# Real parts of eight squarings and two coefficient sums moved from VectorE to float32 identity matmuls on TensorE, with every written-out instruction order replaced

## The chip, the cores and the metric

The kernel runs on one NeuronCore of a Trainium2 chip. The metric is the device time of one execution in microseconds (us). Three executions of the kernel before took 405.08, 403.68 and 402.94 us; the median is 403.68 us. The engines are called by the profile's names: PE (TensorE matmuls, with PEld for weight loads), DVE (VectorE), ACT (ScalarE), POOL (GpSimd) and SP (the queue that issues nearly all DMAs; SPq in the trace).

## The reference

The input x has 2048 rows of 512 values. Four layers follow one another, each added to x after a layer norm: A, B, A, B.

```
x = x + A(layernorm(x));  x = x + B(layernorm(x));  x = x + A(layernorm(x));  x = x + B(layernorm(x))

A: q, k, v = x @ wqkv, 32 heads of 16; each position looks at W = 8 positions, 0, 2, ..., 14 rows back
   softmax over the 8 logits, weighted sum of v, then @ wo
B: dt = exp(log_dt);  A = A_re + i A_im;  Bc, Cc likewise          (512 channels x 128 states)
   P[d,n,l] = exp(dt A[d,n] l),  l = 0..2047
   K[d,l]   = Re sum_n Cc[d,n] P[d,n,l] dt Bc[d,n]
   y = causal convolution of x with K along l (by FFT of length 4096), plus Dskip * x
```

K does not depend on x and is the same in both B layers, so it is made once.

## The kernel before

The work is staged as: generation of K together with the front of the first A layer (function `k_gen`, 0 to about 110 us), the core of the first A layer (`LayerA.core` with l = 0, about 110 to 190 us), the first B layer (`FftB.run` with ORDER0), the front of the second A layer (ORDERF), the core of the second A layer (CORE1) and the second B layer (ORDER1). In each stage a string of letters gives the order in which pieces of work are recorded; a letter calls the next piece of its kind. Each engine executes its own instructions strictly in the recorded order, and waits at the first one whose operands are not ready. SP likewise issues its DMAs one after another in recorded order, so a DMA that is recorded earlier holds up those behind it.

**Generation.** K is formed from powers of z = exp(dt A). The squarings z -> z^2 run for k = 0 to 10: `square(k)` (token s, ACT) squares the real and the imaginary plane into the buffer `ws`; `double(k)` (token i, DVE) makes the new imaginary part 2 re im; `differ(k)` (the next token i, DVE) makes the new real part re^2 - im^2. Planes are 128 x 512 in float32; a z of two planes is the tile `sq_z`, with two buffers. `power(k)` (token b, ACT) copies z to bf16, for k = 3 to 7 into `pow_t` and otherwise into `B_t`; `power_neg` makes the negated imaginary plane. `c_part` (token C) forms the complex product C B in six DVE instructions: for each of the two parts two products into t1 and t2, and one sum into `c_t`. `b_part` (token M) multiplies powers into the table `B_t`, and `levels` (tokens T and U) builds four tables `A_t` from `pow_t`, all on DVE. The products of the tables (token p, PE, line 1268) are copied out by ACT into `kgs` (token x, line 1276). Interleaved with it are the layer norm of x (statistics a, inverse deviation W, applications y and z on ACT and DVE), the transposes of x (token t, PE, line 1196) and the K and Q projections (tokens k and q, PE, line 1206, copied out by ACT under K and Q). When the last `kgs` copy is done, `k_store` sends K to `kd_dram` in 24 DMAs on SP (line 1290).

**Core of an A layer.** m multiplies q with k shifted by the 8 distances (`mult`, DVE, line 342, four per block of rows q = 0 to 3; the first three of layer 0 are done at the end of generation as tokens X); l sums them over a head on PE; x, e, r, n, T are the softmax; v projects V (`v_proj`, PE, line 398, evicted by ACT in line 400) in the order even rows, then odd rows. After the eighth and the sixteenth v, two DMAs (lines 403 and 404) write the shifted rows that later products read:

```
if a >= 14:
    b = a - 14
    nc.sync.dma_start(v[1:113, b:14:2, :], v[0:112, 16 + b:30:2, :])
    nc.sync.dma_start(v[113:128, b:14:2, :], v[112:127, 16 + b:30:2, :])
```

P multiplies the softmax with v (`pv_mult`, DVE, line 467, tile `pav`, one per row in the order 0, 2, 1, 3, 4, ...): row 0 and row 2 read even rows of `v_ext`, row 1 reads odd rows. S and V sum on PE, O is the output projection. Digits and capital letters are events. In layer 0, event 1 is `k_half_load(0)` and event 6 is `k_half_load(1)`: each loads one half of the channels of K back from `kd_dram` into a tile `k_rl` with 18 DMAs on SP (lines 1357 and 1373). In layer 0 the eighth v also starts the four loads of `wo` (line 308) and of the first block of x (line 1455), the sixteenth v those of the other three blocks. The order string of layer 0 before is

```
CORE0 = vmvvvlmqlxmvvvemlvqrlmqvnTmlvxqqlmevlrvmmvvvvnPllPqxmSqTeO0mPlVrP15SOS2PnOPVPOSml4qOOlb3mV78lPPC...
```

so that both events 1 and 6 stand behind the sixteenth v.

Of the kernel before, what the change touches and what calls it, by code (L numbers as in the profile page):

```python
# [10 lines left out]
ACT = mybir.ActivationFunctionType  # L11
ALU = mybir.AluOpType
# [8 lines left out]
P = 128  # L21
# [25 lines left out]
isCbCiCbsiMaiCCbsiMiGGsbcCbMaTMiiMisMbiMbsGbMiGbiMTbcsibTTaiTcbTsbMTiiGbTGGsTMGciaiMTGMcabMGMaTM  # L47
asaMMGMlalTiWMlaaiyTbayiyTMawaMytatMTelkaeMsqMkdliqMaMKMaMMqMqWMlbQQMMMqMyHykUUakpKkyyttkaxUUpKU
kaUUUUaqUUxeUQppqHkdxxKUqeQTkTaUTklqT3paTqlKWTkQTplqkyqx3Ty3QKxT3TTpqlkTpyyHqWEUxktQlKtkUzkekeTK
zUUUkkzkUztKkKtkkTUpexUUKUEkUkeUkUKpKUokxkpxpKUkUxxkqUKEpxoqkkUpUUxopXXXKQpZxxZZ  # L50
"""
ORDER0 = """
KD KA KA KA KD KA KD KA KD KA KD kA KA kD KA KD UA KD UA UA UD KA kA kD kA UD
UA UD UA kD kA kD u UD u u UA m m m UA u u UD u UA m kD UA kD UA m
m u UA u m kA u kD u m kD u kD kA kA yA m YA m yD u yA u m m m
u u yA m m u YA m yA w000D yD yA YD yA w010D YA yD yA
# [3 lines left out]
yA h00 YA h01 v100A v110D h10 a0 z12A p0 z11A n0D h11 w001A w011A S a1 p1 T0 E01A z13A E00D n1G H2  # L60
P02 a2 P00 Q00 p2 T1 E10D E11D P01 P11 P12 n2D H3 a3 P13 T2 P10 E20D E21D P03 p3 P21 P22 n3D
P23 T3 E30D E31A P20 x1
"""
ORDER1 = """
UA UD UA UD UA UA UD UA UD UD u u m m u u m m UA u UA UD m UA u u
UD UA u m m u u m m u YD m u YA YA m u yD m yA u u m m u w001A
m m yA yA w000D YA yD yA YD w011D yA yD w010D yA yD yA v101A v103D v113A v102D v112D v111D v110A v100A
# [919 lines left out]
NROW = 641  # L987


def k_gen(tc, nc, a_consts, ins, kd, la, x_v, lnst, zero, b_consts):  # L990
# [3 lines left out]
    with ExitStack() as ctx:  # L994
# [55 lines left out]
        a_rest()  # L1050
        ws = sp.tile([P, 3, 4 * P], F32, name="ws")
# [3 lines left out]
        cur = {0: sp.tile([P, 2, 4 * P], F32, name="sq_z", tag="sq_z", bufs=2)}  # L1055
        a_re, turn = cur[0][:, 0], ws[:, 2]
# [17 lines left out]
        nc.vector.tensor_tensor(cur[0][:, 1], a_re, sn, ALU.mult)  # L1074
        nc.vector.tensor_tensor(cur[0][:, 0], a_re, cs, ALU.mult)

        def square(k):
            nc.scalar.activation(ws[:, 0:2], cur[k][:], ACT.Square)

        def double(k):  # L1080
            cur[k + 1] = sp.tile([P, 2, 4 * P], F32, name="sq_z", tag="sq_z", bufs=2)
            nc.vector.scalar_tensor_tensor(cur[k + 1][:, 1], cur[k][:, 0], 2.0, cur[k][:, 1], ALU.mult, ALU.mult)

        def differ(k):
            nc.vector.tensor_tensor(cur[k + 1][:, 0], ws[:, 0], ws[:, 1], ALU.subtract)  # L1085

        def planes(k):
            return cur[k][:].rearrange("p r (c x) -> p r c x", c=NCH)
# [4 lines left out]
        def power(k):  # L1093
            copy = copy_by(ENGK["b"][k + max(0, min(k - 3, 5))])
            if 3 <= k <= 7:
                copy(Pw[:, :, k - 3, 1::2, :].rearrange("p c r x -> p r c x"), planes(k))
            else:
                copy(Bt[:, :, :, B_L.index(1 << k), :], cur[k][:].rearrange("p r (q g) -> p r q g", g=4))
# [481 lines left out]
```

## Time and profile before

| what | value |
|---|---|
| time, three executions | 402.94, 403.68, 405.08 us |
| the profiled execution | span 402.6 us from first to last instruction; its own time is not listed beside it |
| DVE busy | 383.5 us, 95% of the span |
| PE busy | 328.0 us (matmul ends are modelled) |
| ACT busy | 321.8 us |
| POOL busy | 59.1 us |
| DVE busy from 10 to 150 us, summed over the windows | 138.4 us of 140 |
| DVE busy from 350 to 402 us | 45.58 us of 52 |

The page gives busy times per engine, the span in 40 slices, the chain of waits that ended last, and the costliest groups of instructions. The trace behind it can be asked for single engines in order of time: start, duration, engine, line, operation, output and inputs. Starts of neighbouring instructions on DVE and ACT are closer together than the listed durations, since one begins while the last one drains: three float32 DVE instructions in a row begin at 9.81, 10.41 and 11.00 us and are listed with 0.67 to 0.68 us each.

### The profile page before, as it was taken

How to read it: one execution, taken by the hardware profiler on the slowest of the kernel's cores; microseconds unless marked ns; L12 is line 12 of the kernel's file. 1: busy time of each engine (PE TensorE's matmuls, PEld its weight loads, DVE VectorE, ACT ScalarE, POOL GpSimd, SP SyncE). 2: the span in 40 equal slices, each digit the busy share in tenths (PEclk: the TensorE clock that was granted, in tenths of full speed). 3: DMA queues.
4: the chain of work that ended last, by engine and by line, in shares of the span. 5: the costliest groups of instructions: out<-in, count | busy, mean ns of one | idle time of the engine just before them, and what ended most of it. 6: DMA issues, size and time to landing. Idle time of an engine off the chain costs nothing.

```text
span 402.6 us, 14781 instructions
## 1 busy us (share of the span) xinstructions
PE 328.0 (81%) x6527; PEld 230.3 (57%) x6527; DVE 383.5 (95%) x460; ACT 321.8 (80%) x557; POOL 59.1 (15%) x75
## 2 busy tenths in 40 slices
PE   3000059999999989999998889999999998997895
PEld 2000026657735656756987888543456666566885
DVE  6999999999999999999999998979899999989994
ACT  7999888898656578988999987674666677989974
POOL 9402400000199500200600000100000001000000
PEclk9999997999999999999999999999999999999999
DMA  7952711115013875259236685730063019504606
GB/s 219 395 143 37 81 52 50 44 27 117 3 43 76 214 210 160 55 173 384 93 112 232 228 285 166 280 114 2 0 170 94 3 39 383 161 2 134 186 14 202
DMA packets 62323, 54.17 MB, mean 135 GB/s; under 512 B 33869, under 2 KB 50738, under 8 KB 60978
## 3 DMA queue, kind: packets, MB, share of 16 engines
q1 hardware_dynamic: 62250, 53.22, 43.5%
q8 instruction: 51, 0.84, 0.9%
q14 instruction: 14, 0.11, 0.1%
q10 hardware_dynamic: 8, 0.00, 0.0%
HBM read 30.15 MB, written 13.24 MB: 108 GB/s over the span
## 4 chain that ended last, share of the span: by engine, by line
PE 36%; DVE 31%; ACT 17%; issue 8%; DMA 5%; SPq 2%; POOL 1%; DVEq 0%; ACTq 0%; POOLq 0%
DVE pav L467 11%; PE pq L398 6%; PE pk L1268 5%; ACT a1s L791 5%; PE pp L1206 4%; DVE t L847 3%; PE pq L223 3%; DVE prod L342 3%; PE pp L282 3%; PE L L350 2%; ACT ub L860 2%; DVE B_t L1110 2%; DVE sq_z L1085 2%; DMA v_ext<-v_ext 2%; DMA kf_ring<-kf_dram 2%
## 5 line engine op out<-in xcount | busy, mean ns | idle before, releaser
L467 DVE TENSOR_TENSOR pav<-attn,v_ext 128x4096 bf16<-128x4096 bf16 (+1 forms) x34 | 72.4, 2168 | 0.4 <-DMA v_ext<-v_ext 0.3
L342 DVE TENSOR_TENSOR prod<-qT,kT_ext 128x4096 bf16<-128x4096 bf16 x29 | 67.0, 2341 | 1.4 <-PE L L350 0.9
L1196 PE MATMUL pt<-ident,x_blk 128*128 128x128 bf16 x64 | 5.9, 241 | 42.8 <-DVE x_blk L197 38.6
L1110 DVE TENSOR_TENSOR A_t<-A_t,pow_t 128x1024 bf16<-128x1024 bf16 (+4 forms) x46 | 38.3, 870 | 0.3
L492 PEld LDWEIGHTS <-pav 64*128 64x128 bf16 x1664 | 26.2, 95 | 13.5 <-DVE pav L467 8.6
L503 PE MATMUL pq<-wop,oT 128*128 128x512 bf16 x128 | 32.9, 379 | 0.7 <-ACT oT L494 0.7
L860 ACT CAST ub<-pb 128x1024 bf16<-128x1024 f32 x32 | 32.1, 1079 | 1.2 <-PE pb L809 1.2
L492 PE MATMUL po<-ident,pav 64*128 64x64 bf16 x1664 | 29.3, 190 | 4.2 <-DVE pav L467 3.2
L400 ACT CAST v_ext<-pq 128x512 bf16<-128x512 f32 x32 | 18.8, 586 | 16.2 <-PE pq L398 16.2
L809 PE MATMUL pb<-a1s,w_sb 128*128 128x64 bf16 x768 | 27.4, 193 | 5.0 <-ACT a1s L791 1.7
L398 PE MATMUL pq<-wv,xnT 128*128 128x512 bf16 x128 | 30.6, 380 | 0.0
L1206 PE MATMUL pp<-xnT,kT_ext 128*128 128x512 bf16 x96 | 27.1, 411 | 4.3 <-ACT kT_ext L1211 2.3
L1196 PEld LDWEIGHTS <-x_blk 128*128 128x128 bf16 x64 | 4.6, 107 | 44.8 <-DVE x_blk L197 38.8
L809 PEld LDWEIGHTS <-w_sb 128*128 128x128 bf16 x768 | 24.9, 98 | 7.2 <-issue 5.2
L791 ACT CAST a1s<-pb 128x1024 bf16<-128x1024 f32 x29 | 28.2, 1059 | 0.8 <-PE pb L802 0.8
L1268 PEld LDWEIGHTS <-A_t 128*64 128x64 bf16 (+1 forms) x512 | 22.9, 107 | 4.5 <-DVE B_t L1110 0.3
L1268 PE MATMUL pk<-B_t,A_t 128*64 128x84 bf16 (+1 forms) x512 | 24.6, 206 | 0.0
L791 DVE CAST a1s<-pb 128x1024 bf16<-128x1024 f32 x19 | 22.6, 1217 | 1.4 <-PE pb L802 1.3
L223 PE MATMUL pq<-xnT,kT_ext 128*128 128x512 bf16 x96 | 23.9, 380 | 0.0
L225 ACT CAST qT<-pq 128x512 bf16<-128x512 f32 x24 | 14.1, 586 | 9.3 <-PE pq L223 9.2
L509 ACT ACTIVATE x_sb<-pq 128x512 bf16<-128x512 f32 x24 | 14.3, 594 | 8.7 <-PE pq L503 8.7
L398 PEld LDWEIGHTS <-xnT 128*128 128x128 bf16 x128 | 11.6, 98 | 15.3 <-issue 3.0
(259 smaller groups left out, 897.0 us busy)
## 6 DMA issues: line engine op xcount, KB each, us to landing
w_sb<-w_dram SPq DMA_DIRECT2D x8, 1024.0 KB, 7.8
w_dram<-xnT SPq DMA_DIRECT2D x1, 4096.0 KB
kf_ring<-kf_dram SPq DMA_DIRECT2D x13, 256.0 KB, 4.8
kf_ring<-kf_dram SPq DMA_DIRECT2D x26, 128.0 KB, 4.3
v_ext<-v_ext SPq DMA_DIRECT2D x4, 784.0 KB, 6.6
x_blk<-in_A_x_dram SPq DMA_DIRECT2D x4, 512.0 KB, 4.1
kT_ext<-in_A_wqkv_dram SPq DMA_DIRECT2D x4, 512.0 KB, 9.2
x_sb<-in_A_x_dram SPq DMA_DIRECT2D x4, 512.0 KB, 5.3
```

Of the source, the lines that this page charges most:

```text
L223: nc.tensor.matmul(pq[:], lhsT=self.wqk[:, dt, ft * P:(ft + 1) * P], rhs=self.xnT[:, dt, q * 512:(q + 1) * 512], start=(dt == 0), stop=(dt ...
L342: nc.vector.tensor_tensor(pr, self.qT[q][:, ft].unsqueeze(1).to_broadcast([P, W, 4, P]), kap, ALU.mult)
L398: nc.tensor.matmul(pp[:], lhsT=xnT[:, dt, a * P:(a + 1) * P], rhs=wv[:, dt, :], start=(dt == 0), stop=(dt == NDT - 1))
L467: nc.vector.tensor_tensor(pv[:, i], attn[:, n % 4].unsqueeze(2).to_broadcast([P, W, DH // parts, H]), vap, ALU.mult)
L492: nc.tensor.matmul(po[:, h, 0, i * nt + ft, :], lhsT=pvf[rows, i, w, ft * P:(ft + 1) * P], rhs=ident[rows, rows], start=(w == 0 and ft + i ...
L503: nc.tensor.matmul(pw[:], lhsT=oT[:, ftp, :], rhs=self.wo[:, ftp, :], start=False, stop=(ftp == NDT - 1))
L791: (self.nc.scalar.copy if eng == "act" else self.nc.vector.tensor_copy)(dst, src)
L809: nc.tensor.matmul(p2[:, j, :], lhsT=self.w2[:, ec * EC + j, :], rhs=a1s[:, ec * EC + j, :], start=True, stop=True)
L860: nc.scalar.copy(ub[:], p2)
L1110: return lambda: nc.vector.tensor_tensor(*args)
L1206: nc.tensor.matmul(pps[kind, b, ft][:], lhsT=la.wqk[:, dt, c:c + P], rhs=la.xnT[:, dt, b * 512:(b + 1) * 512], start=(dt == 0), stop=(dt = ...
L1268: nc.tensor.matmul(o, lhsT=lhs, rhs=Bt[:, ri, c * CH + ql].rearrange("p b g -> p (b g)"), start=(not half and j % 4 == 0 and ri == 0), sto ...
```

## The change

The real part of the squarings with k = 3 to 10 is formed on PE. `ws` holds the two squares in float32; a float32 identity times the first and a negated float32 identity times the second are accumulated in one PSUM bank, and that bank is the real plane from then on. So `square`, `power` and `double` read the real plane from PSUM and the imaginary one from SBUF, and what was one ACT instruction over both planes becomes two. For the first three squarings nothing changes. The two sums of `c_part` are made in the same way, with an ACT copy to `c_t` behind each; the second pair of products is written to a part of `kT_ext`. The two float32 identities are made by POOL behind its other start-up work. The six raw input tiles now lie in the two q tiles (their DMAs are the same, in the same order), and `sq_z` has separate rings for one and two planes.

All order strings are new. The number of pieces of each kind, and the engine of each, are the same as before in every string. In CORE0, event 6 (the load of one half of K) now stands before the odd v, and in the built program its 18 DMAs stand on SP ahead of the two that shift the odd rows of `v_ext`.

```diff
 ORDERK = """
+siCCbisbiisCCCiibsMGCiiMbMMMMsibbbMTMicMMcsabbiisTTbbTTTTiiccTaiGTTsbGbGTTTibMMMasGiiGGaacGaTGMM
+GGbMMMMasallMMMMaaMTaaiiaaMaWlbsMMMaiyyyyilltWbweMMMMMMMMtdkHeqlyyqUUUkUKpUUyykkpQkkKxtaxkkKtpaK
+UUUdapaaUUqqUUUHxaaTTTqq3TTx33l3TTEppQQalTTeeTqWqqQqqQxxqqqllTTQQTTpkyyyypkkkHKKWUUUtxxtekkUelUU
+kkppKKxxzzzzkkkpEKkUUUttkKkepKekkkkUKUUUExxUUUUUUUkKkpokkKKoqoqQXXkkxpKpxpZZXZxx
 """
...
 CORE0 = """
-vmvvvlmqlxmvvvemlvqrlmqvnTmlvxqqlmevlrvmmvvvvnPllPqxmSqTeO0mPlVrP15SOS2PnOPVPOSml4qOOlb3mV78lPPC
-SOdxS6eOrPSPPOSnwaOPSBPOSaOS9bOfAPdbFPOtVftEGDSaafaOH
+vvvmmlvvmxqqllev0vrmmlvvlnTmvmvvvll6xeqPPvvvqqrmmS3lnVlOOqqmx1TPP4qS2SOOm5P7llPVemmSO8PBrCPllbVx
+nOOeSPPrSOnSP9POOASPSOSPPOdSOaaffVbwbOPttdEaaSfaHOGDF
 """
 CORE1 = """
-0m1l2ml3mvvqlmvlvqmxmqvlqqvemllvmrqvlnmTmqxqlmvvelvvvvmPvPqvrlnlTqSmOSxmPqlPeSPOmSOSlOPrlSOqPSPO
-SnmPOOlbxSOPePVbPrdSnPdfOVfaOPwSfPOSfOSbafOPdfaSttfaOa
+0vml12mqmlq3vlqmmlxvvlemmvvrnlqqqlvmTmlqqlxmmvqvlvvmlmevvrvvvPSPlnqOxqSmTOPPlSPOSlSeqOPOrPSSmmlb
+POOSdnPfflOxSePafbVPPdrOnSOVPPfOSPOSbaOPSfdtOfaSfatOaw
 """
...
+SQ_PE = 3
...
         raw = {}
+        q0, q1 = (la.qT[b][:].rearrange("p t a q -> p (t a q)") for b in range(2))
         for name in ("A_im", "A_re", "B_re", "B_im", "C_re", "C_im"):
-            raw[name] = sp.tile([P, 4, N], BF16, name="raw_" + name)
-            nc.sync.dma_start(raw[name][:], ins[name].rearrange("(t p) n -> p t n", p=P))
+            home = (q0, q1)[len(raw) // 4]
+            raw[name] = home[:, len(raw) % 4 * 512:(len(raw) % 4 + 1) * 512].rearrange("p (t n) -> p t n", n=N)
+            nc.sync.dma_start(raw[name], ins[name].rearrange("(t p) n -> p t n", p=P))
...
         a_rest()
+        ident32 = sp.tile([P, P], F32, name="ident32")
+        nident32 = sp.tile([P, P], F32, name="nident32")
+        nc.gpsimd.tensor_copy(ident32[:], ident[:])
+        nc.gpsimd.tensor_copy(nident32[:], la.c["nident"][:])
...
         def square(k):
-            nc.scalar.activation(ws[:, 0:2], cur[k][:], ACT.Square)
+            if k <= SQ_PE:
+                nc.scalar.activation(ws[:, 0:2], (im[k] or z0)[:], ACT.Square)
+                return
+            for r in range(2):
+                nc.scalar.activation(ws[:, r], cur[k][r], ACT.Square)
 
         def double(k):
-            cur[k + 1] = sp.tile([P, 2, 4 * P], F32, name="sq_z", tag="sq_z", bufs=2)
-            nc.vector.scalar_tensor_tensor(cur[k + 1][:, 1], cur[k][:, 0], 2.0, cur[k][:, 1], ALU.mult, ALU.mult)
+            z = sp.tile([P, 1 if k >= SQ_PE else 2, 4 * P], F32, name="sq_z", tag=f"sq_z{k >= SQ_PE}", bufs=2)
+            nc.vector.scalar_tensor_tensor(z[:, 0 if k >= SQ_PE else 1], cur[k][0], 2.0, cur[k][1], ALU.mult, ALU.mult)
+            im[k + 1] = z
 
         def differ(k):
-            nc.vector.tensor_tensor(cur[k + 1][:, 0], ws[:, 0], ws[:, 1], ALU.subtract)
+            if k < SQ_PE:
+                cur[k + 1] = im[k + 1][:, 0], im[k + 1][:, 1]
+                nc.vector.tensor_tensor(cur[k + 1][0], ws[:, 0], ws[:, 1], ALU.subtract)
+                return
+            re = pst.tile([P, 4 * P], F32, name="pt")
+            nc.tensor.matmul(re[:], lhsT=ident32[:], rhs=ws[:, 0], start=True, stop=False)
+            nc.tensor.matmul(re[:], lhsT=nident32[:], rhs=ws[:, 1], start=False, stop=True)
+            cur[k + 1] = re[:], im[k + 1][:, 0]
 
         def power(k):
...
+            for r, z in enumerate(cur[k]):
+                if 3 <= k <= 7:
+                    copy(Pw[:, :, k - 3, 1 + 2 * r, :], z.rearrange("p (c x) -> p c x", c=NCH))
+                else:
+                    copy(Bt[:, r, :, B_L.index(1 << k), :], z.rearrange("p (q g) -> p q g", g=4))
...
+        def c_sum(q, t):
+            pc = pst.tile([P, 4 * P], F32, name="pt")
+            nc.tensor.matmul(pc[:], lhsT=ident32[:], rhs=t[0], start=True, stop=False)
+            nc.tensor.matmul(pc[:], lhsT=(ident32 if q else nident32)[:], rhs=t[1], start=False, stop=True)
+            nc.scalar.copy(c0[:, q], pc[:])
+
+        prods = [(t1[:], t2[:]), [la.kT[:, 3, a:a + 8, :].rearrange("p a q -> p (a q)").bitcast(F32) for a in (14, 22)]]
+
         def c_part():
-                yield tt(nat(t1[:]), T[x0], T[y0], ALU.mult)
-                yield tt(nat(t2[:]), T[x1], T[y1], ALU.mult)
-                yield tt(c0[:, q], t1[:], t2[:], op)
+                t = prods[q]
+                yield tt(nat(t[0]), T[x0], T[y0], ALU.mult)
+                yield tt(nat(t[1]), T[x1], T[y1], ALU.mult)
+                yield lambda: c_sum(q, t)
```

ORDERK before, and the strings ORDER0, ORDERF and ORDER1, which are new as well, are left out of this cut.

More of the change, by code (lines that the diff above doesn't have):

```diff
@@ L1054, in k_gen @@
         t2 = sp.tile([P, 4 * P], F32, name="t2")
-        cur = {0: sp.tile([P, 2, 4 * P], F32, name="sq_z", tag="sq_z", bufs=2)}
-        a_re, turn = cur[0][:, 0], ws[:, 2]
+        z0 = sp.tile([P, 2, 4 * P], F32, name="sq_z", tag="sq_zFalse", bufs=2)
+        cur = {0: (z0[:, 0], z0[:, 1])}
+        a_re, turn = cur[0][0], ws[:, 2]
         p_im = turned_by("A_im", by_dt)
@@ L1110, in tt @@
             return lambda: nc.vector.tensor_tensor(*args)
-        def c_part():
-            for q, (x0, y0, x1, y1, op) in enumerate((("C_re", "B_re", "C_im", "B_im", ALU.subtract),
-                                                      ("C_re", "B_im", "C_im", "B_re", ALU.add))):
-                yield tt(nat(t1[:]), T[x0], T[y0], ALU.mult)
-                yield tt(nat(t2[:]), T[x1], T[y1], ALU.mult)
-                yield tt(c0[:, q], t1[:], t2[:], op)
+        def c_sum(q, t):
[4 more added lines that the diff above has]
+        prods = [(t1[:], t2[:]), [la.kT[:, 3, a:a + 8, :].rearrange("p a q -> p (a q)").bitcast(F32) for a in (14, 22)]]
+        def c_part():
+            for q, (x0, y0, x1, y1) in enumerate((("C_re", "B_re", "C_im", "B_im"), ("C_re", "B_im", "C_im", "B_re"))):
+                t = prods[q]
+                yield tt(nat(t[0]), T[x0], T[y0], ALU.mult)
+                yield tt(nat(t[1]), T[x1], T[y1], ALU.mult)
+                yield lambda: c_sum(q, t)
         def bmul(src, by, dst):
```

45 lines of the change are left out of this document (21 added, 24 removed).

## The prediction

> **What bounds the kernel now.** I read the page first, then the groups of the first 110 us by shape, then the single engines in order of time: POOL and ACT around 13 us, SP from 100 to 200 us, DVE from 98 to 150 us.
>
> ```profile
> PE 328.0 (81%) x6527; PEld 230.3 (57%) x6527; DVE 383.5 (95%) x460; ACT 321.8 (80%) x557; POOL 59.1 (15%) x75
> DVE  6999999999999999999999998979899999989994
> ACT  7999888898656578988999987674666677989974
> ```
>
> DVE is the bound of nearly the whole span; in generation ACT is almost as full (slices 2 to 5). So work taken off DVE counts only while nothing else makes DVE wait.
>
> ```profile
> L1085 DVE TENSOR_TENSOR sq_z<-ws 128x512 f32<-128x512 f32 x11 | 7.5, 683 | 0.1
> L1110 DVE TENSOR_TENSOR c_t<-t,t 128x512 bf16<-128x512 f32 x2 | 1.5, 728 | 0.0
> L1078 ACT ACTIVATE ws<-sq_z 128x1024 f32<-128x1024 f32 x11 | 11.5, 1048 | 0.0
> L1098 ACT CAST B_t<-sq_z 128x1024 bf16<-128x1024 f32 x7 | 7.3, 1039 | 1.4 <-DVE sq_z L1085 1.2
> ...
> 60.96 2.72 PE pp L1206 x6
> ...
> 69.27 0.97 PE pp L1206 x4
> ```
>
> The first four lines are what the change edits (duration of one in ns before the last bar). The last two, from the chain of waits, are the nearest prices for the new matmuls: a bf16 matmul of 512 columns takes 2.72/6 = 0.45 us where the windows show a granted clock of 0.50 (60 to 66 us) and 0.97/4 = 0.24 us where they show 1.00.
>
> ```profile
> 14.06 0.52 POOL L128 TENSOR_SCALAR slot_mask<-iota_slot_mask 4x16 bf16<-4x16 int32 x1
> ...
> 110.01 16.16 SPq L1290 DMA_DIRECT2D kd_dram<-kgs  x24
> 127.55 0.69 SPq L403 DMA_DIRECT2D v_ext<-v_ext  x1
> 128.29 0.94 SPq L404 DMA_DIRECT2D v_ext<-v_ext  x1
> 129.28 4.08 SPq L308 DMA_DIRECT2D wop<-in_A_wo_dram  x4
> 133.40 0.59 SPq L1455 DMA_DIRECT2D x_sb<-in_A_x_dram  x1
> 137.07 0.64 SPq L403 DMA_DIRECT2D v_ext<-v_ext  x1
> 142.12 0.61 SPq L1357 DMA_DIRECT2D k_rl<-kd_dram  x1
> 142.78 12.49 SPq L1373 DMA_DIRECT2D k_rl<-kd_dram  x17
> ...
> 103.41 6.69 DVE L342 TENSOR_TENSOR A_pr<-qT,kT_ext 128x4096 bf16<-128x4096 bf16 x3
> 135.75 4.89 DVE L467 TENSOR_TENSOR pav<-attn,v_ext 128x4096 bf16<-128x4096 bf16 x2
> 146.10 6.68 DVE L467 TENSOR_TENSOR pav<-attn,v_ext 128x4096 bf16<-128x4096 bf16 x3
> ```
>
> Call E the end of the last kgs copy (110.0) and X the start of the first logit product on DVE (103.4). SP does nothing useful for the attention until its 24 stores of K are out: the even rows of v_ext start at E+17.5 and, with the 6.9 us to landing that the DMA view gives, are there at E+24.9, just before the first pav (135.75 = E+25.7). The odd rows are issued at E+27 and are there before the third pav (146.1).
>
> **The change part by part.** *DVE, generation.* Eight subtractions and two sums go. Their starts lie 0.60 us apart, so 10 x 0.60 = 6.0 us (6.9 by listed durations). Nothing is added; a product read from PSUM already costs the same (0.68).
>
> *ACT, generation.* One 1024-wide instruction takes 0.95 us start to start; two of 512 take 0.49 (from PSUM, lines 1072) and 0.52. That is +0.06 for each of 7 squares and 8 power copies, and two copies to c_t add 0.98: +1.9 us in all.
>
> *PE, generation.* Twenty float32 matmuls of 512 columns, in ten pairs; no row shows one. Lower end: one warm bf16 row each, 0.48 a pair. Upper end: each operand is twice as wide as any that PE is given here, so four part products at the cold row, 8 x 0.45 = 3.6 a pair. I take 2.8, between four warm (1.9) and four cold (3.6), because PE ran cold from 60 to 66 us after pauses of 1 to 2 us and the pairs will have such pauses. The Trainium skill, page "FP8 and Floating Point Precision", TensorE Precision Notes, gives float32 four passes, which no run here shows; by it my upper end is the price of a cold pair.
>
> *What waits for the pairs.* In the built order ACT's first c_t copy stands ahead of the power of z^4 and the fourth square, and needs the identities that POOL makes behind slot_mask, ready by about 15.2 and 15.7 us (two instructions like ident, 0.56). The pair then ends at 15.2+2.8 = 18.0; ACT is free at 14.7: a wait of 3.3. Then each square waits for the pair of the square before. From the start of one first-half square its pair begins 0.6 later, so a step is at least 3.4 us; where ACT has less of its own work between two squares it waits: 0.9 before square 4, 0.4 before 5, 0.8 before 6, none after. DVE's doubling waits for that first-half square too (both read the same bank): 2.9 before doubling 4, 1.6 before doubling 7, and 1.5 in the first steps. So DVE idles about 6.0 there against 1.6 before, and X = 103.4 - 6.0 + 4.4 = 101.8. ACT, whose queue up to the first x_blk application adds up to 40.6 us from 9.6, comes to it at 50.2 + 6 = 56.2 (48.15 before, though 4 statistics, a square and a copy that followed it then are now done), and the last pair, before the transposes on PE, ends at 58.0 (the transposes ran from 51.8 before).
>
> *E after.* By DVE: behind the last table step PE has 12 projection matmuls (2.9) and four product groups of 1.37, then 0.75 for the copy: E = 101.8 + 9.2 = 111.0. By PE: from 51.8 to 109.2 it holds 45.4 us of warm work (64 transposes 3.6, 96 projections 20.7, 16 product groups 21.1) and about 5 of cold clock and waits: 58.0 + 50.4 + 0.1 = 108.5. I take E = 110, no earlier than before; the saving is spent on the waits. With 1.9 a pair the same walk gives E = 107.5, with 0.48 106.5, with 3.6 115 (transposes at 64, X 106.8).
>
> The Trainium skill, page "TensorE: Matmul & The Clock Gate", Part 1, says the clock opens after about 3.4 us of steady work and closes after an idle window of that length; this trace agrees in size (0.50 from 60 to 66 us, 1.00 from 67). Were the pairs steady enough to stay warm by it, E would be 107.5 and the time 2.5 us under my forecast.
>
> *Core of layer A0: SP.* Event 6 is moved ahead of the odd v. SP now issues after the even rows: wo (4.08), one block of x (0.59), then the 18 loads of k_rl, at 0.65 + 11.5 to 12.5 (the trace has 17 in 12.49 with waits for x_sb inside, and 11.52 in the second set), and only then the odd rows: E + 17.5 + 1.7 + 4.1 + 0.6 + 12.7 = E + 36.6, landing E + 43.5 (E + 34 before). DVE is there earlier: the first pav now comes 25.5 us of DVE work after X (two logit products and one normalization fewer ahead of it than before), the third 12.7 later. With X = 101.8 and E = 110 it waits for the even rows from 127.3 to 134.9, 7.6 us, and for the odd rows from 147.6 to 153.5, 5.9 us. The third pav is 7.4 later than before, and one product (2.2) that stood before it is now behind it. From there DVE was busy without a gap to about 190 us, so A0 ends 9.6 later. The load itself is hidden in both orders; what is late is what stands behind it.
>
> *Core of layer A1.* Before the sixteenth v PE now has one more lsum and one more reciprocal sum (0.55 + 0.45) and waits beside them; the third pav there waited for this v_ext (0.31 idle at 311.19): +1.4.
>
> *ORDER0, ORDERF, ORDER1.* The same pieces on the same engines. Their DVE idle is 1.6 (200 to 250), 3.5 (250 to 300) and 6.4 us (350 to 402); a new order can win part of it or add as much. I take 0 and keep -6 to +4.
>
> *At no cost.* The raw tiles in q: the same six DMAs in the same place; the q tiles are first written by the projections at 60 us. The two identities: POOL is idle from 14.6 to 38.2 us; their lateness is the wait above. The second pair of products in kT_ext: written at 58 us at the earliest otherwise.
>
> Sum: 402.6 + 9.6 + 1.4 = 413.6; the median of the runs lies 1.1 above the profiled span, so 414.7. Forecast 414.5.
>
> **The rivals.** *Pairs stay cold (3.6).* For it: the pauses. Against it: two sums and the first squaring follow each other from 15 us almost without one. E = 115: the third pav at 158.5, 402.6 + 14.6 + 1.4 + 1.1 = 419.7.
>
> *Pairs are cheap and the late orders win.* E = 106.5 gives 411.2, less up to 6 from the idle of the last stages: 405 to 411. For it: DVE's idle is there to be filled. Against: part of the idle at the end is behind kf_ring loads (3.17 and 2.99 us in the chain).
>
> *Faster: generation comes forward by more than the SP queue costs.* Its place is PE before the products: kept warm from 15 us on, it works through 45.4 us without the 5 of cold clock and waits, and the DVE saving of 6.0 arrives whole. It decides where E falls below 99 (then 43.5 + 2.2 + 1.4 after E is no later than before). With E = 95 the time is 399.7. Against it: X cannot be under 97.4 by DVE's own work, four product groups follow, so E is hardly under 103.
>
> *Change without effect on the end:* the waits and the saving cancel and v_ext is not what the third pav waits for; against it stands the built order, in which that pav waits for just these two DMAs.
>
> **How the numbers follow.** Forecast case (E 107.5 to 112) 0.58, cold pairs 0.15, cheap pairs with gains later 0.14, faster 0.08, no effect 0.05. What lies within 0.5% (2 us), about what a measurement of this kernel can tell from no change, is the last. Slower: 0.58 + 0.15 + 0.14 = 0.87; same 0.05; faster 0.08. The range 404 to 421 leaves out the faster case and the far end of the cold one.
>
> **What would show it.** Right: SP's L1373 loads directly behind x_sb and ahead of the second pair of v_ext copies; DVE idle some 6 us or more before the first pav (even rows) and again before the third (odd rows); ACT idle near 15 us before the first c_t copy; ten pairs of about 2.8 us; E at 108 to 112. Wrong: E near 100, a third pav before 146 us, or float32 pairs under 1 us; or a last stage that gives back more than 6 us.

## The result: 418.55 us, 3.8% slower, and the profile after

Beside each other the changed kernel took 418.55 us (median of four executions, 417.27 to 422.6) and the kernel before 404.32 us (402.94 to 405.08): ratio 1.0376, 95% interval 1.0346 to 1.0406. The forecast was 414.5 us, slower, with a range of 404 to 421. The profiled execution after is the one of 417.27 us; its span is 415.5 us, 12.9 more than the span before. Every execution is 1.7 to 1.8 us longer than its span.

The page after: busy time per engine, and the rows of DVE, ACT and PE's granted clock (the share of its full speed that PE was given, in tenths) over the 40 slices (about 10.4 us each).

```profile
PE 348.9 (84%) x6525; PEld 239.5 (58%) x6567; DVE 379.0 (91%) x450; ACT 324.3 (78%) x574; POOL 51.0 (12%) x77
DVE  6989999999996959999999999989997989989994
ACT  7799999997566468869999997575666468889982
PEclk9998879999999889999999999999999899999998
```

DVE has ten instructions and 4.5 us less to do and is slower at it: its share falls from 95% to 91%. The holes are the thirteenth and the fifteenth slice (125 to 135 and 145 to 156 us); both were full before. The row of the clock has two long dips, at 31 to 62 us and at 135 to 156 us; before, it held 9 in all slices but the seventh (60 to 70 us, 7).

DVE's costliest group after, and one group of the new matmuls (mean duration of one in ns before the last bar, then idle time of the engine in front and what ended most of it):

```profile
L466 DVE TENSOR_TENSOR pav<-attn,v_ext 128x4096 bf16<-128x4096 bf16 (+1 forms) x34 | 72.2, 2161 | 12.2 <-DMA v_ext<-v_ext 11.1
L1103 PE MATMUL pt<-ws,ident 128*128 128x512 f32 x16 | 11.3, 798 | 18.0 <-ACT ws L1090 17.1
```

Of DVE's idle time 11.1 us stand before products that wait for `v_ext`, 9.3 of them in A0 and 1.8 in A1. SP's queue after, in order of time (start, duration, line, count):

```profile
109.14 15.52 SPq L1323 DMA_DIRECT2D kd_dram<-kgs  x24
126.05 0.69 SPq L402 DMA_DIRECT2D v_ext<-v_ext  x1
126.78 0.94 SPq L403 DMA_DIRECT2D v_ext<-v_ext  x1
127.78 4.19 SPq L307 DMA_DIRECT2D wop<-in_A_wo_dram  x4
132.01 0.59 SPq L1488 DMA_DIRECT2D x_sb<-in_A_x_dram  x1
132.65 0.56 SPq L1390 DMA_DIRECT2D k_rl<-kd_dram  x1
133.25 10.71 SPq L1406 DMA_DIRECT2D k_rl<-kd_dram  x17
144.07 0.64 SPq L402 DMA_DIRECT2D v_ext<-v_ext  x1
144.76 0.92 SPq L403 DMA_DIRECT2D v_ext<-v_ext  x1
...
148.91 0.60 SPq L734 DMA_DIRECT2D g_dram<-k_perm  x1
149.56 0.61 SPq L1390 DMA_DIRECT2D k_rl<-kd_dram  x1
150.21 11.61 SPq L1406 DMA_DIRECT2D k_rl<-kd_dram  x17
161.92 3.03 SPq L734 DMA_DIRECT2D g_dram<-k_perm  x3
```

DVE around the first and the third `pav`, after (the bracket is the idle time in front and what ended it):

```profile
132.90 4.49 DVE L466 TENSOR_TENSOR pav<-attn,v_ext 128x4096 bf16<-128x4096 bf16 x2 [4.15 <-DMA v_ext<-v_ext]
137.31 4.48 DVE L341 TENSOR_TENSOR prod<-qT,kT_ext 128x4096 bf16<-128x4096 bf16 x2
...
151.23 4.49 DVE L466 TENSOR_TENSOR pav<-attn,v_ext 128x4096 bf16<-128x4096 bf16 x2 [5.13 <-DMA v_ext<-v_ext]
155.64 2.28 DVE L341 TENSOR_TENSOR prod<-qT,kT_ext 128x4096 bf16<-128x4096 bf16 x1
```

The 18 loads of `k_rl` stand directly behind `x_sb` and ahead of the odd `v_ext` copies, and DVE waits 4.15 and 5.13 us before the first and the third `pav`. One more thing in SP's queue matters later: the second 18 loads stand ahead of the last three stores of `g_dram`.

Where the 12.9 us of span arise, read from the starts of the same DVE instructions in both traces:

| point | before | after | difference |
|---|---|---|---|
| first logit product of A0 (X) | 103.4 | 101.5 | -1.9 |
| first store of K on SP (E) | 110.0 | 109.1 | -0.9 |
| third `pav` of A0 | 146.1 | 151.2 | +5.1 |
| last `pav` of A0 | 186.0 | 193.1 | +7.1 |
| first logit product of A1 | 268.6 | 277.2 | +8.6 |
| last `pav` of A1 | 349.8 | 361.7 | +11.9 |
| end of the span | 402.6 | 415.5 | +12.9 |

### The profile page after: what moved, and what is told of

Read it like the earlier page. It is cut to its first block, busy times and chain, and to the rows that moved or that the text cites. A ratio compares the mean times of both kernels' runs of the same rounds, so it can differ in the third digit from the quotient of the medians.

```text
span 415.5 us, 14837 instructions
## 1 busy us (share of the span) xinstructions
PE 348.9 (84%) x6525; PEld 239.5 (58%) x6567; DVE 379.0 (91%) x450; ACT 324.3 (78%) x574; POOL 51.0 (12%) x77
## 4 chain that ended last, share of the span: by engine, by line
PE 43%; DVE 27%; ACT 13%; issue 7%; DMA 5%; POOL 3%; SPq 2%; DVEq 0%; ACTq 0%; POOLq 0%
DVE A_t L1135 6%; PE pq L397 6%; PE pq L502 4%; PE po L491 4%; DVE pav L466 4%; PE pq L222 3%; PE pk L1301 3%; PE pp L1239 3%; DMA v_ext<-v_ext 3%; DVE B_t L1135 3%; ACT ub L859 3%; PE pp L281 2%; PE po L481 2%; PE L L349 2%; DVE t L846 2%
## 5 line engine op out<-in xcount | busy, mean ns | idle before, releaser
L466 DVE TENSOR_TENSOR pav<-attn,v_ext 128x4096 bf16<-128x4096 bf16 (+1 forms) x34 | 72.2, 2161 | 12.2 <-DMA v_ext<-v_ext 11.1
L341 DVE TENSOR_TENSOR prod<-qT,kT_ext 128x4096 bf16<-128x4096 bf16 x29 | 65.5, 2292 | 2.2 <-PE L L349 1.1
L491 PEld LDWEIGHTS <-pav 64*128 64x128 bf16 x1664 | 27.6, 97 | 17.2 <-issue 8.4
L491 PE MATMUL po<-ident,pav 64*128 64x64 bf16 x1664 | 30.5, 194 | 8.3 <-DVE pav L466 4.6
L397 PE MATMUL pq<-wv,xnT 128*128 128x512 bf16 x121 | 29.6, 379 | 0.4 <-issue 0.2
L1103 PE MATMUL pt<-ws,ident 128*128 128x512 f32 x16 | 11.3, 798 | 18.0 <-ACT ws L1090 17.1
L1239 PE MATMUL pp<-xnT,kT_ext 128*128 128x512 bf16 x88 | 23.0, 380 | 3.1 <-ACT xnT L1232 1.3
L493 ACT CAST oT<-po 128x512 bf16<-128x512 f32 x26 | 15.0, 579 | 11.7 <-PE po L491 11.6
L1301 PEld LDWEIGHTS <-A_t 128*64 128x64 bf16 (+1 forms) x512 | 21.7, 103 | 3.7
L1301 PE MATMUL pk<-B_t,A_t 128*64 128x84 bf16 (+1 forms) x512 | 23.5, 201 | 0.0
L508 ACT ACTIVATE x_sb<-pq 128x512 bf16<-128x512 f32 x24 | 14.2, 591 | 10.8 <-PE pq L502 10.2
L224 ACT CAST qT<-pq 128x512 bf16<-128x512 f32 x24 | 13.9, 584 | 8.8 <-PE pq L222 8.8
L397 PEld LDWEIGHTS <-xnT 128*128 128x128 bf16 x128 | 11.9, 98 | 14.7 <-issue 1.7
```

The source lines that it names most:

```text
L341: nc.vector.tensor_tensor(pr, self.qT[q][:, ft].unsqueeze(1).to_broadcast([P, W, 4, P]), kap, ALU.mult)
L397: nc.tensor.matmul(pp[:], lhsT=xnT[:, dt, a * P:(a + 1) * P], rhs=wv[:, dt, :], start=(dt == 0), stop=(dt == NDT - 1))
L466: nc.vector.tensor_tensor(pv[:, i], attn[:, n % 4].unsqueeze(2).to_broadcast([P, W, DH // parts, H]), vap, ALU.mult)
L491: nc.tensor.matmul(po[:, h, 0, i * nt + ft, :], lhsT=pvf[rows, i, w, ft * P:(ft + 1) * P], rhs=ident[rows, rows], start=(w == 0 and ft + i ...
L1239: nc.tensor.matmul(pps[kind, b, ft][:], lhsT=la.wqk[:, dt, c:c + P], rhs=la.xnT[:, dt, b * 512:(b + 1) * 512], start=(dt == 0), stop=(dt = ...
L1301: nc.tensor.matmul(o, lhsT=lhs, rhs=Bt[:, ri, c * CH + ql].rearrange("p b g -> p (b g)"), start=(not half and j % 4 == 0 and ri == 0), sto ...
```

## The experiments

All ratios are to the kernel before, run on the same chip; us are medians. Twelve kernels follow, in three steps: which part carries the loss, why giving back one wait gave back no time, and what is left.

### Which part: generation or orders

`gen_only` is the changed kernel, its ORDERK included, with the five other strings of before; `orders_only` is the kernel before with those five strings of after (two of the five, cut short):

```diff
# gen_only: the other five strings of before in the changed kernel; orders_only: the other way round
-CORE0 = "vvvmmlvvmxqqllev0vrmmlvvlnTmvmvvvll6xeqPPvvvqqrmmS3lnVl..."
+CORE0 = "vmvvvlmqlxmvvvemlvqrlmqvnTmlvxqqlmevlrvmmvvvvnPllPqxmSqTeO0mPlVrP15SOS2..."
-CORE1 = "0vml12mqmlq3vlqmmlxvvlemmvvrnlqqqlvmTmlqq..."
+CORE1 = "0m1l2ml3mvvqlmvlvqmxmqvlqqvemllvmrqvlnmTm..."
# and ORDER0, ORDERF, ORDER1 in the same way
```

> The new generation (code and ORDERK) with the other five order strings of the kernel before. Theory 1: the last kgs copy ends near 109 us as in the changed kernel and the first logit product starts near 101.5; with the old CORE0 DVE reaches the first pav near 133.8, just after the even rows land (132.9), so DVE keeps the 1.9 us and the time is 402.4, 1.9 under the 404.3 of before. Theory 2: the generation part carries the loss, the time is 410 to 417.

Measured: 403.6 us, 1.0003 [0.9981, 1.0025]. The generation costs nothing and wins nothing; neither theory's time came. X comes 1.5 us earlier than before (101.9), the first `pav` 0.6 earlier (135.1) and the third 0.6 earlier (145.5); at the first `pav` of A1 both kernels stand at 300.3 us. Part of these differences is spread between executions: four more kernels below keep the generation of before (`orders_only`, `late_orders`, `six_early`, `warm_early`), and in their profiles X lies at 102.6 to 102.7 and E at 109.1 to 109.3, against 100.9 to 101.9 and 108.6 to 109.6 in the nine with the new one. So the new generation brings X forward by about 1 us, and E not at all.

> The kernel before with its own generation and ORDERK, and the other five order strings of the changed kernel. Theory 1: the orders carry the whole loss: last kgs copy near 110, third pav near 152, end of the first core 8.2 later than before, the second core and the front of the second layer add 5 more, 417.5 to 419. Theory 2: the orders are about even, 403 to 406.

Measured: 420.18 us, 1.0403 [1.0359, 1.0446]. The strings alone carry the whole loss, 1.2 us more than theory 1 allowed. The interval overlaps that of the kernel after, so whether the new generation takes any of the loss back is not shown.

`late_orders` splits the strings: the kernel before with CORE1, ORDER0, ORDERF and ORDER1 of after, CORE0 as before.

```diff
-CORE1 = "0m1l2ml3mvvqlmvlvqmxmqvlqqvemllvmrqvlnmTm..."
+CORE1 = "0vml12mqmlq3vlqmmlxvvlemmvvrnlqqqlvmTmlqq..."
# and ORDER0, ORDERF, ORDER1 in the same way
```

> The kernel before with CORE1, ORDER0, ORDERF and ORDER1 of after; generation and CORE0 as before. By the two traces the parts behind the first A layer cost 1.1 + 3.3 + 1.0 = 5.4 us in after: 409.2 (408 to 410.5). By the prediction (1.4 in the second A layer, 0 in the FFT strings) 405.2. If the loss behind the first A layer is only its late end carried on, 403.8.

Measured: 407.69 us, 1.0089 [1.0053, 1.0125]: 3.6 us, more than the 1.4 of the prediction and less than the 5.4 read from two traces (the interval allows 2.1 to 5.1). By the starts of `pav` in its profile, 2.2 us arise between the last of A0 and the first of A1, 0.2 within A1 and 1.1 behind it. No single wait carries it: behind 200 us DVE has 1.3 us before `kT_ext` (0.4 before), 0.9 for POOL's `ln_rstd` (none before), 0.8 for `v_ext` in A1 (0.3 before). With generation at nothing, and if the parts add up, some 10.6 of the 14.2 us belong to CORE0.

### Event 6, alone and undone

`six_early` is the kernel before with event 6 alone moved ahead of the odd v (behind the thirteenth v, where the new CORE0 has it); the rest of that string is unchanged. `six_back` is the kernel after with event 6 moved behind the odd v.

```diff
# six_early (kernel before)
-vmvvvlmqlxmvvvemlvqrlmqvnTmlvxqqlmevlrvmmvvvvnPllPqxmSqTeO0mPlVrP15SOS2PnOPVPOSml4qOOlb3mV78lPPC
-SOdxS6eOrPSPPOSnwaOPSBPOSaOS9bOfAPdbFPOtVftEGDSaafaOH
+vmvvvlmqlxmvvvemlvqrlmqvnTmlvxqqlmevlrvmmv6vvvnPllPqxmSqTeO0mPlVrP15SOS2PnOPVPOSml4qOOlb3mV78lPP
+CSOdxSeOrPSPPOSnwaOPSBPOSaOS9bOfAPdbFPOtVftEGDSaafaOH
# six_back (kernel after)
-vvvmmlvvmxqqllev0vrmmlvvlnTmvmvvvll6xeqPPvvvqqrmmS3lnVlOOqqmx1TPP4qS2SOOm5P7llPVemmSO8PBrCPllbVx
+vvvmmlvvmxqqllev0vrmmlvvlnTmvmvvvllxeqPPvvv6qqrmmS3lnVlOOqqmx1TPP4qS2SOOm5P7llPVemmSO8PBrCPllbVx
```

> The kernel before with one letter moved: event 6 from behind the sixteenth v to behind the thirteenth. Theory 1: the odd rows of v_ext land 42.1 us after the last kgs copy, as in the changed kernel, so the third pav starts at 152.1 instead of 146.1 and the time rises by 6.0 to 410.3. Theory 2: the queue of SP is hidden, 404 to 405.

Measured: 415.29 us, 1.0278 [1.025, 1.0307]: 11.2 us from one letter, where theory 1 expected 6.0. Two lines of SP in `six_early`, the loads of event 6 ahead of the odd copies:

```profile
134.18 11.36 SPq L1373 DMA_DIRECT2D k_rl<-kd_dram  x17
145.66 0.64 SPq L403 DMA_DIRECT2D v_ext<-v_ext  x1
```

The third `pav` in its DVE timeline, and one of the waits behind it:

```profile
143.15 2.28 DVE L342 TENSOR_TENSOR prod<-qT,kT_ext 128x4096 bf16<-128x4096 bf16 x1
153.22 4.49 DVE L467 TENSOR_TENSOR pav<-attn,v_ext 128x4096 bf16<-128x4096 bf16 x2 [7.79 <-DMA v_ext<-v_ext]
...
182.25 2.29 DVE L467 TENSOR_TENSOR pav<-attn,v_ext 128x4096 bf16<-128x4096 bf16 x1 [0.87 <-PE po L492]
```

A wait of 7.79 us at the predicted place moves the third `pav` by 7.1 us. The last `pav` of A0 is 9.9 us late (196.0 against 186.0): behind the wait DVE stands four more times, 2.7 us in all, for PE, which the expectation had not counted.

> The changed kernel with event 6 alone moved back, to directly behind the sixteenth v of CORE0, so that its 18 loads of K stand behind the two DMAs for the odd rows of v_ext. Theory 1 (the SP queue holds the third pav): the 5.13 us that DVE waited there in the changed kernel go, the third pav starts near 146 us instead of 151.2, and the time falls by 5.1 us from 418.6 to 413.4; the 4.15 us before the first pav stay. Theory 2 (the float32 pairs and what they delay are the loss): the odd rows are not what counts, the time stays within 1.5 us of 418.6.

Measured: 420.36 us, 1.0417 [1.0384, 1.0451]; no gain. The wait before the third `pav` is gone (it starts at 147.0, 4.2 us sooner than after), and all of it is lost again: the last `pav` starts at 194.4, after the change at 193.1. So the theory that this wait sets the end of A0 in the new CORE0 fell, although the same load in the old order costs 11 us. DVE in `six_back` now waits for PE and ACT instead (lines from its timeline):

```profile
145.85 1.23 DVE L413 TENSOR_REDUCE mx<-L 128x128 bf16<-128x1024 f32 x1 [0.75 <-PE L L331]
...
171.72 0.69 DVE L447 TENSOR_TENSOR attn<-ex,rs 128x1024 bf16<-128x1024 bf16 x1 [1.24 <-ACT rs L439]
176.83 2.29 DVE L466 TENSOR_TENSOR pav<-attn,v_ext 128x4096 bf16<-128x4096 bf16 x1 [2.03 <-PE po L491]
```

### The first thing behind the wait: PE's clock

In the new CORE0 PE has nothing between the sum of the first `pav` and the next logit sum. The windows of `six_back` over 136 to 148 us (the columns are length, busy us of PE, PEld, DVE, ACT and POOL, granted clock, DMA share, GB/s), and, in the second fence, two lines of its PE timeline:

```profile
136.00:140.00 4.00, 0.86 (x60) 0.73 (x52) 4.00 (x2) 3.01 (x4) 0.00 (x0) 1.00 1.02 239
140.00:144.00 4.00, 3.85 (x61) 3.85 (x62) 4.00 (x4) 0.00 (x0) 0.00 (x0) 0.50 1.01 316
144.00:148.00 4.00, 3.78 (x45) 2.35 (x45) 3.25 (x3) 0.59 (x1) 0.00 (x0) 0.50 0.57 124
```

```profile
140.15 1.02 PE L353 MATMUL L<-ind,prod 128*128 128x8 bf16 x32 [3.30 <-DVE prod L341]
141.03 3.57 PE L481 MATMUL po<-ident,pav 128*128 128x128 bf16 x32
```

After a pause of 3.30 us the granted clock is 0.50 up to about 150 us, and 32 wide sums take 3.57 us that take 1.95 at 1.00 (160.34 us in the same trace). The kernel after has the same pause (3.23 us) and a clock of 0.57 from 140 to 144. `warm_back` and `warm_early` fill such pauses with matmuls whose result nobody reads, into a bank of the projections:

```diff
+            def keep_busy(count):
+                pp = pq_tile()
+                for i in range(count):
+                    nc.tensor.matmul(pp[:], lhsT=xnT[:, i % NDT, 0:P], rhs=wv[:, i % NDT, :], start=True, stop=True)
# warm_back: six_back with, at the end of pv_sum
+                if l == 0 and n == 0:
+                    keep_busy(14)
# warm_early: six_early with, at the start of pv_sum
+                if l == 0 and n == 1:
+                    keep_busy(34)
```

> The kernel after with event 6 behind the odd v, as in six_back, and 14 extra matmuls of 512 columns on PE behind the first sum of pav (nothing reads them). In six_back PE has a pause of 3.3 us there (136.9 to 140.2), its granted clock is 0.50 from 140 to 148 and 0.72 to 152, and the 32 wide sums that take 1.95 us elsewhere take 3.57. Theory C, the clock: the 4.2 us that the third pav gained are lost because PE then works at half clock; kept busy it stays at 1.00, the waits on PE and ACT behind 147 us go, and the time is 416.5 (415.5 to 418, against 420.4 of six_back). Theory O, the order: PE and ACT have the same chain of work at any clock in the new CORE0; the time stays within 1.2 us of 420.4.

Measured: 418.27 us, 1.0349 [1.0321, 1.0377], 2.1 us under `six_back` by the medians, half of what theory C asked for; the two intervals are just apart. The clock is 1.00 from 132 to 168 us and the third `pav` starts 1.0 us sooner, as expected; but in the profiled execution (the slowest of its four, where that of `six_back` is the fastest) the last `pav` is where it was (194.3), because ACT then stands for something else:

```profile
169.47 1.04 ACT L1490 COPY k_perm<-k_rl 128x1024 bf16<-128x1024 bf16 x1 [6.09 <-DMA g_dram<-k_perm]
```

Behind this wait PE has a pause of 5.26 us, and its clock is 0.50 from 172 to 176 us.

> The kernel before with event 6 alone moved ahead of the odd v, as in six_early, and 34 extra matmuls of 512 columns on PE ahead of the sum of the third pav (nothing reads them), to fill 8 us of the 9.1 us in which PE stands there. In six_early the clock is 0.50 to 0.73 from 148 to 160 and DVE then waits four times for PE, 2.7 us in all. Theory C: these waits go and the time is 412.6 (411.8 to 413.6), 2.7 under the 415.3 of six_early. Theory O: the waits come from the changed spacing of products and sums; the time stays within 1 us of 415.3.

Measured: 413.03 us, 1.0239 [1.0196, 1.0281]. The intervals of `six_early` and `warm_early` overlap, so the times do not settle it. The traces do as to the mechanism: the clock stays at 1.00 from 144 to 184 us (0.73, 0.50, 0.50 from 148 to 160 without the filling), DVE's waits for PE behind the third `pav` fall from 2.7 to 0.9 us, and the last `pav` starts at 193.5 instead of 196.0.

### The second thing: the stores of g_dram

The wait of ACT in `warm_back` comes from SP's order too. The first bf16 copies of K into `k_perm` overwrite a buffer that the four stores of `g_dram` read. In the new CORE0 both loads of K (events 6 and 1) stand ahead of events 4, 2 and 5, which issue three of these stores; in the old one event 6 stands behind all four. SP in `warm_back`:

```profile
140.08 13.56 SPq L1413 DMA_DIRECT2D k_rl<-kd_dram  x17
153.75 0.56 SPq L741 DMA_DIRECT2D g_dram<-k_perm  x1
154.36 0.62 SPq L1397 DMA_DIRECT2D k_rl<-kd_dram  x1
155.02 10.81 SPq L1413 DMA_DIRECT2D k_rl<-kd_dram  x17
165.93 1.94 SPq L741 DMA_DIRECT2D g_dram<-k_perm  x3
```

All 36 loads of K are issued ahead of the last three stores. The trace of `six_back` has the same order and a shorter wait before the same copy:

```profile
170.12 1.04 ACT L1483 COPY k_perm<-k_rl 128x1024 bf16<-128x1024 bf16 x1 [2.82 <-DVE ln_rstd L176]
```

The profile puts it down to an instruction of DVE that had ended 0.8 us sooner. That it was a store, issued at 165.33, is likely and not shown. `ext_act` shows the wait for the stores again, longer. It is the kernel after with the four `v_ext` copies of A0 issued by ACT:

```diff
-                    nc.sync.dma_start(v[1:113, b:14:2, :], v[0:112, 16 + b:30:2, :])
-                    nc.sync.dma_start(v[113:128, b:14:2, :], v[112:127, 16 + b:30:2, :])
+                    (nc.sync if l else nc.scalar).dma_start(v[1:113, b:14:2, :], v[0:112, 16 + b:30:2, :])
+                    (nc.sync if l else nc.scalar).dma_start(v[113:128, b:14:2, :], v[112:127, 16 + b:30:2, :])
```

> The kernel after with the four v_ext copies of the first A layer issued by ACT, right behind the v that they follow, in place of SP. Theory 1, SP's queue: what holds up the first and the third pav (4.15 and 5.13 us) is only that SP comes late to these copies; both waits go, PE has no pause and no closed clock, and the time is 418.6 - 9.3 = 409.3 (408 to 412). ACT pays for four issues, at most 2.8 us at SP's price, beside DVE. Theory 2, the rest of the new CORE0: DVE gains at most as much as in six_back, since sums and evictions bind behind the third pav; 415 or more.

Measured: 420.39 us, 1.0397 [1.0371, 1.0423]. Theory 1 missed by 11 us; the 415 or more of theory 2 holds. The first `pav` still waits 2.93 us, for another DMA into `v_ext` (`v_ext<-rows`, line 535) that stayed on SP behind the stores of K. The third `pav` does start at 144.7, 6.5 us sooner than after, without a wait; the clock is 1.00 up to 164 us. Then ACT stands, and A0 with it:

```profile
173.02 1.04 ACT L1483 COPY k_perm<-k_rl 128x1024 bf16<-128x1024 bf16 x1 [10.91 <-DMA g_dram<-k_perm]
...
174.27 0.31 ACT L439 ACTIVATE rs<-ssum 128x128 bf16<-128x128 f32 x1
```

The attention is sooner at this copy and the stores are later: they start at 169.26 on SP (161.92 after), because its first 17 loads take 18.51 us there in place of 10.71, 9.1 of them in a wait for the `v_ext` copies. DVE waits 5.4 us for the `rs` behind that copy, 3.6 us for PE and 2.7 us for a load of K.

`gen_ext_act` does the same edit on `gen_only`.

> The new generation with the five other strings of before (gen_only, 403.6) and the four v_ext copies of the first A layer issued by ACT. Theory 1: the 2 us that DVE comes earlier to the first logit product are lost only because SP is busy with the stores of K until E + 17.5; the first pav comes at 133.8 in place of 135.1 and the time is 402.3 (401.5 to 403). Theory 2: behind the first pav something else is already late (PE sums, evictions); 403.2 to 404.2, no difference.

Measured: 406.26 us, 1.0056 [1.0039, 1.0073], by the ratios 2.1 us worse than `gen_only`; both theories missed. The first `pav` stays at 135.0, without a wait for `v_ext` in either kernel, so it was not waiting for the even copies. ACT issues the odd copies when it has evicted the last v (136.87 and 137.57; SP issued them at 136.67 and 137.35 in `gen_only`) and is then held 2.20 us in front of its next eviction. The third `pav` waits 2.01 us for `v_ext`, at 147.0: the odd copies were issued only 0.2 us later, but took 9.5 us to landing, where `gen_only` shows 6.1. Why they took longer stays open.

`sp_order` puts both loads where SP had them before: event 1 right behind the odd v, event 6 behind event 5. `sp_order_warm` adds the 14 matmuls of `warm_back`.

```diff
-vvvmmlvvmxqqllev0vrmmlvvlnTmvmvvvll6xeqPPvvvqqrmmS3lnVlOOqqmx1TPP4qS2SOOm5P7llPVemmSO8PBrCPllbVx
+vvvmmlvvmxqqllev0vrmmlvvlnTmvmvvvllxeqPPvvv1qqrmmS3lnVlOOqqmxTPP4qS2SOOm56P7llPVemmSO8PBrCPllbVx
```

> The kernel after with both loads of K in CORE0 placed as SP had them before: event 1 right behind the odd v, event 6 behind event 5, so that SP issues the odd v_ext copies, one set of 18 loads, the four stores of g_dram, the other set. Theory S, a second queue of the same kind: in after and six_back all 36 loads stand ahead of the last three g_dram stores (165 to 167 us in six_back), and ACT's k_perm copies wait for these with out-projection evictions and sums behind them; once that is gone, 4 us of what six_back lost come back: 416.4 (415 to 417.5), and no ACT wait on g_dram. Theory C alone, the clock: PE's pause at 137 to 140 is unchanged, the time stays within 1.2 us of the 420.4 of six_back.

Measured: 416.59 us, 1.033 [1.0264, 1.0396]; its four executions lie far apart (413.44 to 419.87), and the interval overlaps that of `six_back`. The value is the one expected (416.4), and in the profiled execution, the fastest of the four, ACT no longer waits for `g_dram` and the last `pav` starts at 189.5.

> sp_order with the 14 extra matmuls of warm_back behind the first sum of pav. Theory S with C: in warm_back the clock stayed at 1.00, DVE came 1.0 us sooner to the third pav, and then ACT stood 6.1 us for the g_dram stores and DVE 6.3 us in two waits behind ACT; with the stores early these go and the time is 418.3 - 6 = 412.3 (411 to 414). If the back half is bound by the order of sums and evictions itself, 416.5 or more.

Measured: 414.19 us, 1.0251 [1.0182, 1.0319] (411.72 to 417.74), 412.3 expected. Against `six_back` (1.0384 at the least) the two edits together win 6.2 us by the medians, and the intervals are apart. The profiled execution, again the fastest, has the last `pav` at 188.7 and a clock of 1.00 from 132 to 184 us. So what holds `six_back` up includes both, the clock, shown in its own trace, and the order of the stores, shown in `warm_back` and `ext_act`; how much belongs to each the times leave open.

### What is left: the first pav

In `sp_order_warm` DVE still waits 3.83 us before the first `pav` (132.79): the new CORE0 has less DVE work ahead of it. `cover_first` is `sp_order` with two logit products and two projections moved ahead of it.

```diff
-vvvmmlvvmxqqllev0vrmmlvvlnTmvmvvvllxeqPPvvv1qqrmmS3lnVl...
+vvvmmlvvmxqqllev0vrmmlvvlnTmvmvvvllxeqqqmmPPvvv1rS3lnVl...
```

> sp_order with two more pieces of work ahead of the first products in CORE0: the two logit products that followed the first two pav, and the two projections that they read, now stand before them. Theory W: what is left of the loss in the first A layer is DVE's wait of 4.3 us before the first pav, which the new order leaves without cover, and PE's pause behind it, which closes the clock; both go, the odd rows of v_ext come 2 us later and hold the third pav up by about 1, and the time is 416.6 - 4.3 - 2.4 + 1 = 410.9 (409.5 to 413). Theory O: DVE gets there without a wait, but sums and evictions behind it bind: 414.5 or more.

Measured: 414.71 us, 1.0259 [1.024, 1.0279], 1.9 us under `sp_order` by the medians, not distinguishable from it by the intervals, and 3.8 us more than theory W asked for; the 414.5 or more of theory O holds. The first `pav` starts without a wait, but the wait has moved: the waits of DVE from 110 to 200 us in the profiled execution (at 417.71 us the slowest of seven):

```profile
DVE prod L341 <- ACT qT L224: 3.2, 2, 2.6
DVE pav L466 <- PE po L491: 3.1, 3, 2.4
DVE mx L413 <- PE L L331: 2.1, 1, 2.1
```

2.6 us are spent on the projection that was moved up with the products, and PE's pause is now in front of the sum of the first `pav` (2.7 us), with a clock of 0.50 from 140 to 148 us again. None of the twelve kernels is faster than the kernel before. Of the 10.1 us that `sp_order_warm` still loses against it (404.1 beside it), 3.6 are the late strings by `late_orders`, if the parts add up; what in CORE0 makes up the other 6.5, beside the wait before the first `pav`, stays open.

## Why the prediction was right, and where its steps were off

**Sign and size.** Slower was right, and the place, A0 behind SP's queue, too: `orders_only` (1.0403) and `gen_only` (1.0003) confirm that the orders decide, `six_early` that event 6 ahead of the odd rows is enough for most of a loss of this size (11.2 of 14.2 us). Measured 418.55 against the sum of 414.7: 1.9 us of the gap are in the span (12.9 against 11.0 predicted), 1.3 in the profiled execution being the fastest of its four, 0.7 in the 1.1 us put between span and median, which is 1.8 between span and time.

**Generation.** X at 101.5 (101.8 predicted), last pair ending at 58.0 (58.0), E at 109.1 (110), ACT's wait before the first `c_t` copy 2.88 us (3.3). X came out by two misses that cancel: up to it DVE's busy time fell by 4.6 us (92.32 to 87.75, counted from 9.56 us on), not by 6.0, and its idle time rose from 1.53 to 4.16 us, not to 6.0. Of the waits worked out for the squarings, ACT shows none before squares 4 to 6, and DVE 1.86 us before doubling 4 (2.9) and none before doubling 7 (1.6). The price of a pair, 2.8, was a mean of two values that both occur. PE in the first pairs and the last one, after:

```profile
13.99 2.08 PE L1139 MATMUL pt<-t,ident 128*128 128x512 f32 x2 [6.90 <-POOL ident L1055]
15.86 1.65 PE L1140 MATMUL pt<-t,nident 128*128 128x512 f32 x2
17.35 1.02 PE L1139 MATMUL pt<-kT_ext,ident 128*128 128x512 f32 x2
18.20 1.02 PE L1140 MATMUL pt<-kT_ext,ident 128*128 128x512 f32 x2
...
54.19 2.08 PE L1103 MATMUL pt<-ws,ident 128*128 128x512 f32 x2 [6.62 <-ACT ws L1090]
56.06 1.91 PE L1104 MATMUL pt<-ws,nident 128*128 128x512 f32 x2
```

Cold means at half clock here. One float32 matmul of 512 columns, listed as two records, takes 1.87 us from start to start in these two cold pairs and 0.85 to 0.97 in a warm one: to its listed end a pair takes 3.5 to 3.8 or 1.9 to 2.0 us, about four times the bf16 rows (0.45 and 0.24 each) in both cases. Four of the ten pairs are cold (the first and the last three), six warm. The upper end of the prediction was right for the cold ones, its four warm rows (1.9) for the others. The four passes for float32 that the Trainium skill gives (page "FP8 and Floating Point Precision", TensorE Precision Notes) agree with this factor. The identities were ready at 13.9 and 14.2 us, 1.3 and 1.5 sooner than worked out, and the first pair was cold, so the two errors nearly cancelled in ACT's wait. (The clock of that pair is not in this trace, which reads 1.00 up to 37 us; `six_back`, whose first pair took as long, shows 0.50 from 13 to 17 us.) The last three pairs ran cold, with pauses of up to 6.6 us ahead of them (clock 0.88, 0.78 and 0.66 in the windows of 10 us from 30 to 60 us). The rival "pairs stay cold" priced these four rightly and got E wrong (115): from 30 to 60 us DVE was busy 9.8 to 9.9 us of each 10, and PE waited for the others, not they for it.

**SP's queue.** The 18 loads stood where they were predicted and took 11.3 us (12.7 predicted); the odd copies were issued at E + 35.0 (36.6), and the third `pav` came at E + 42.1 (43.5). With the earlier E this is 151.2 instead of 153.5: +5.1 and not +7.4. The waits were 4.15 and 5.13 us (7.6 and 5.9), the first one smaller because DVE got there at 128.75, not 127.3, and the even rows landed 2 us sooner. One product behind instead of ahead is the other 2.2, 7.3 in all: the last `pav` of A0 was 7.1 late, 9.6 predicted. So far the path is the one forecast.

**The step that holds in this kernel alone: "From there DVE was busy without a gap".** The prediction let A0 end by DVE's work behind the third `pav`, and in the kernel after it did. `six_back` and `ext_act` show that this holds only while the wait stands: without it PE's clock and the `g_dram` stores take its place. By the terms of the prediction the kernel with event 6 moved back would be some 5 us faster, and `six_back` is not. So the forecast names a path that is there, and it comes near the time partly by luck: it had no term for two losses that set the end of A0 once this wait is gone. One is the stores: "the load itself is hidden in both orders" was true of what the loads feed, and not of the three stores behind all 36 of them, for which ACT waits 6.1 us in `warm_back` and 10.9 in `ext_act`; in the kernel after a single wait of 0.60 us is put down to them. The other is the clock. The rule that it closes after an idle window (the Trainium skill, page "TensorE: Matmul & The Clock Gate", Part 1) was weighed for generation, where it moved no end, and not for the core, where the waits that were forecast make just such pauses; it closed behind pauses of 2.68 (`cover_first`), 3.23 and 3.30 us here, and of 1.83 us in `ext_act` (0.50 from 165.5 us), all less than the page's figure for that window. The kernel before had shown this: its clock closed at 59 us behind a pause of 2.01 us, so the prediction's "agrees in size" holds for the stretch at half clock and not for the pause ahead of it.

**Behind A0.** 1.4 us were put on A1 and 0 on the FFT strings (ORDER0, ORDERF, ORDER1). The wait behind the 1.4 is there: the third `pav` of A1 waits 1.79 us for `v_ext` after, 0.31 before. `late_orders` measures 3.6 for all four strings, and by its profile nearly all of it outside A1's products (2.2 ahead of them, 1.1 behind). So what was put at 0 cost some 3.3 us, inside the -6 to +4 that was kept, and on its bad side. The rival in which the late orders win is out.

## What to carry to other kernels

When a DMA is moved up in one queue, read everything that is issued behind it and ask of each who waits: here one letter put 18 loads ahead of two copies, which cost 11 us, and the order of two letters put 36 loads ahead of three stores, a loss hidden behind the first. A wait that is taken away gives back only the distance to the next wait, so before crediting a gain look for the engine that has to be on time there, and for the buffer that it writes. A wait forecast for DVE can be a pause of PE too, as it was here, and its price then includes the half clock behind it.

## What the runs showed of the hardware that was not expected

A pause of 2.7 to 3.3 us in PE's records was enough for a granted clock of 0.50 over the next 3.4 us (after) to 10 us (`cover_first`, `six_back`), while pauses of at most 1.2 us left it at 1.00 in A0 before; 14 dummy matmuls in the pause (an estimate of 3.4 us at 0.24 each) kept it open. The length of one pause does not settle it: 1.83 us in `ext_act` (before 165.43) were followed by 0.50, and 2.09 us in the kernel after (before 32.61) by 1.00. The 128 x 128 bf16 to float32 casts of the identities took POOL 0.28 us each, half of what was taken. Issuing four copies from ACT instead of SP cost 2.1 us (`gen_ext_act`): the two odd issues held ACT's queue 0.67 and 1.03 us, its next eviction began 2.20 us after the last one, and the copies took longer to land; which of these the time comes from is not shown.
